# Float64 weights to float32 by a Prelu on ScalarE, with one VectorE operation a piece fewer

## The chip, the cores and the metric

One core of a Trainium2 chip runs the whole program. The metric is the device time of one execution in microseconds. Times of several runs are given by their median.

## The reference

The reference is a chain of three layers on 4 sequences of 576 tokens. The first is attention with 8 heads of 64 in a window of 32 keys (dilated by 4 in half of the heads). The second mixes with phases, the third is a gated unit whose gate runs over the tokens:

```python
theta = x @ w_theta
zr, zi = x * cos(theta), x * sin(theta)
u = x + w_tok_r @ zr + w_tok_i @ zi          # over the tokens
x = u + maximum(u @ w_ch, 0)
h = maximum(x @ w_in, 0); u, v = halves of h
v_n = (v - mean(v)) / sqrt(var(v) + 1e-6)
out = (u * (w_spatial @ v_n + b_spatial)) @ w_out
```

q, k, v, w_spatial and b_spatial are float32. w_theta, w_tok_r, w_tok_i, w_ch, w_in and w_out arrive as float64 and have to be brought to float32 on the chip.

## The kernel before

Matrix products run as float32r in three terms: each operand is split into a high part and a low part, and high x high, low x high and high x low are summed in PSUM. So each weight goes through three steps: float64 to float32 (bits64), a rounded copy as the high part, and a subtraction for the low part (split_weight, which L144 ends).

bits64 takes a piece of 128 rows by 256 or 288 columns. A DMA on SP's queue brings the 64-bit words to SBUF (four buffers named w64; w_theta has buffers of its own, wth64). The high words, read as float32 with a step of two, are multiplied by 2^-112, which moves the exponent to where float32 wants it (L128 on ScalarE or L130 on GpSimd, by a letter in a table). VectorE then does three operations: L131 shifts the low words right by 29 into c, which lies in PSUM; L132 shifts the scaled word left by 3 and ors c into it, again into c; L133 keeps the sign bit of the scaled word and ors c into it.

The letters of IN_ENG, SP_ENG, OUT_ENG, TOK_ENG, CH_ENG and THETA_ENG (L53 to L57) say which engine makes the high part, which the low part, and, as a third letter, which scales in bits64 (GpSimd where there is none). ScalarE scales the first half of w_tok (9 pieces), w_ch (8) and w_out (8); GpSimd scales w_theta (8), the second half of w_tok (9) and w_in (16).

The program is written as generators that are interleaved, and a scheduler in the tile framework then sets the order of the instructions on each engine; each engine's queue runs in that order. The stages are: attention of batch 0 (scores L250, exps L265, division L268 on GpSimd, transposes L278, their copies L280, values L292 and L296, and copies of the result into x, L299 to L308), with the w_theta pieces among it; the theta units of batch 0 (th_unit: xh L350, xl L353, twelve matmuls L358, ta L366, L367, Sin L375 and L376, products L379, then zh and zl by split, zl at L330 on GpSimd), with the first half of w_tok among them; token mixing of batch 0 (tm_run, L429 and L436) together with attention of batch 1, the second half of w_tok and w_ch; channel mixing (ch_run, L455); the same for the other batches with w_in among them; then the second half (hv_unit L650, hu_run L695, sp_run L714 to L717, out_unit L743), at whose start the w_out pieces are converted among the layer norms.

The tables and the place where w_theta is queued:

```python
IN_ENG, SP_ENG, OUT_ENG = "vgg", "ag", "aga"
TOK_ENG = ("aga", "gv")
CH_ENG = "vga"
THETA_ENG = "gg"
```

Of the kernel before, what the change touches and what calls it, by code (L numbers as in the profile page):

```python
# [11 lines left out]
F32 = mybir.dt.float32  # L12
# [3 lines left out]
AF = mybir.ActivationFunctionType  # L16
ALU = mybir.AluOpType
# [32 lines left out]
HELD = 2  # L50


IN_ENG, SP_ENG, OUT_ENG = "vgg", "ag", "aga"  # L53
TOK_ENG = ("aga", "gv")
CH_ENG = "vga"
THETA_ENG = "gg"
Z_HI = ("v", "g")  # L57

# [5 lines left out]
def tile_block(ctx: ExitStack, tc: tile.TileContext, qT, kT, vw, eye_in, mask_in, eye_b_in, w_theta, w_tok, w_ch, w_in, w_sp, w_sph, b_sp, w_out, out):  # L64
    nc = tc.nc
    V, A, G, PE, SY = nc.vector, nc.scalar, nc.gpsimd, nc.tensor, nc.sync

    def f32(ap):
        return ap.bitcast(F32)
# [34 lines left out]
    def copy(dst, src, eng):  # L104
        if eng == "a":
            A.copy(dst, src)  # L106
        elif eng == "v":
            V.tensor_copy(dst, src)
        else:
            G.tensor_scalar(dst, src, 1.0, 1.0, op0=ALU.mult, op1=ALU.mult)  # L110

    last_dma = [None]

    def bits64(src, n, eng, st=None):

        p = src.shape[0]
        if st is None:
            st = const.tile([P, 2 * CH], U32, tag="w64", name="w64", bufs=4)  # L120
        last_dma[0] = SY.dma_start(st[:p, :2 * n], src.bitcast(U32))
        w = st[:p, :2 * n].rearrange("p (n w) -> p n w", w=2)
        lw, hw = w[:, :, 0], w[:, :, 1]
        g = const.tile([P, CH], F32, tag="stage", name="w64g", bufs=4)[:p, :n]
        c = c64[:p, :n].bitcast(U32)
        gi = g.bitcast(U32)
        if eng == "a":
            A.mul(g, hw.bitcast(F32), 2.0**-112)  # L128
        else:
            G.tensor_scalar(g, hw.bitcast(F32), 2.0**-56, 2.0**-56, op0=ALU.mult, op1=ALU.mult)  # L130
        V.tensor_scalar(c, lw, 29, None, op0=ALU.logical_shift_right)  # L131
        V.scalar_tensor_tensor(c, gi, 3, c, op0=ALU.logical_shift_left, op1=ALU.bitwise_or)  # L132
        V.scalar_tensor_tensor(gi, gi, 0x80000000, c, op0=ALU.bitwise_and, op1=ALU.bitwise_or)  # L133
        return g

    def split_weight(src, hi, lo, eng_hi, eng_lo, eng_bits="g", st=None):
        n = hi.shape[-1]
        if src.dtype == F32:
            s = const.tile([P, CH], F32, tag="stage", name="stage", bufs=4)[:src.shape[0], :n]
            SY.dma_start(s, src)  # L140
        else:
            s = bits64(src, n, eng_bits, st)
        copy(hi, s, eng_hi)
        (G if eng_lo == "g" else V).tensor_tensor(lo, s, f32(hi), op=ALU.subtract)  # L144

    def halves(src, hi, lo, k, n, engs):

        for c in range(2):
            cs = slice(n // 2 * c, n // 2 * (c + 1))
            split_weight(src[:, k, cs], hi[:, k, cs], lo[:, k, cs], *engs)  # L150

    def stored(src, dst, k, cs, engs):

        n = cs.stop - cs.start
        t = const.tile([P, 2, CH], F32R, tag="parts", name="parts", bufs=2)[:, :, :n]
        split_weight(src[:, k, cs], t[:, 0], t[:, 1], *engs)
        SY.dma_start(f32(dst[:, k, :, cs]), f32(t))

    def w_theta_job(k, c):
        cs = slice(DM // 2 * c, DM // 2 * (c + 1))  # L160
        split_weight(w_theta[:, k, cs], wth_h[:, k, cs], wth_l[:, k, cs], *THETA_ENG, st=pz.tile([P, DM], U32, tag=f"z{'hl'[c]}{k}", name="wth64"))

    def w_tok_job(k, c):
        cs = slice(CH * c, CH * (c + 1))
        split_weight(w_tok[:, k, cs], wtok_h[:, k, cs], wtok_l[:, k, cs], *TOK_ENG[c])

    wch = []

    def w_ch_job(k):
        if not wch:  # L170
            wch.extend(p1.tile([P, 4, DM], F32R, tag=n, name=n) for n in ("wch_h", "wch_l"))
        halves(w_ch, *wch, k, DM, CH_ENG)

# [392 lines left out]
    n = 0  # L566
# [272 lines left out]
```

## Time and profile before

| | us |
|---|---|
| median of 3 runs | 552.2 |
| lowest and highest run | 551.26, 556.32 |
| span of the profiled execution | 552.0 |
| TensorE busy in it | 533.7 |
| VectorE busy | 318.1 |
| ScalarE busy | 246.1 |
| GpSimd busy | 262.9 |

The profiled execution is one of its own; the page gives its span, from the first instruction to the last, and no other time of it. The median of the runs stands 0.2 us above that span. In the profile's rows PE is TensorE, DVE is VectorE, ACT is ScalarE, POOL is GpSimd, SP is the engine whose queue issues DMAs. A time in brackets is the engine's idle time ahead of the instruction, with what ended it.

### The profile page before, as it was taken

The page shows a single profiled execution, that of the slowest core. Times are in us where ns is not written, and L with a number is a line of the kernel's source. Part 1 is how long each engine was busy: PE and PEld are TensorE (multiplying, and loading weights), DVE is VectorE, ACT ScalarE, POOL GpSimd, SP SyncE. Part 2 cuts the span into 40 slices and gives each one's busy share as a digit, 9 for nine tenths or more (in the row PEclk, how much of TensorE's full clock was granted, in tenths as well). Part 3 has the DMA queues.
Part 4 walks back from the last instruction along what each step waited for, and adds up shares of the span by engine and source line. Part 5 has one row for each costly group of instructions (what it writes and reads, how often), then busy time and mean ns, then how long its engine had stood idle before and what let it go on. Part 6 is the DMA issues. An engine that isn't in the chain of part 4 may idle for free.

```text
span 552.0 us, 11197 instructions
## 1 busy us (share of the span) xinstructions
PE 533.7 (97%) x4148; PEld 476.6 (86%) x4148; DVE 318.1 (58%) x834; ACT 246.1 (45%) x718; POOL 262.9 (48%) x333
## 2 busy tenths in 40 slices
PE   6897989999999999999999999989999999999997
PEld 4674878888989988889889999989899889988996
DVE  2688999899778378762782143984602148253020
ACT  4769855535655444772560124742422233233222
POOL 3484996554995249820296328563302204322040
PEclk9979899999999999999999999999999999999999
DMA  8925755662378552630006968250015110002002
GB/s 217 288 74 151 212 156 169 192 191 80 94 233 244 129 179 93 212 96 2 0 1 215 371 210 267 94 170 3 21 57 172 58 38 1 2 1 77 1 0 96
DMA packets 43759, 67.16 MB, mean 122 GB/s; under 512 B 3764, under 2 KB 26552, under 8 KB 43704
## 3 DMA queue, kind: packets, MB, share of 16 engines
q1 hardware_dynamic: 43480, 66.26, 39.0%
q8 instruction: 33, 0.54, 0.4%
q10 hardware_dynamic: 224, 0.18, 0.1%
q14 instruction: 22, 0.18, 0.1%
HBM read 48.08 MB, written 18.35 MB: 120 GB/s over the span
## 4 chain that ended last, share of the span: by engine, by line
PE 71%; DVE 10%; DMA 6%; ACT 5%; issue 4%; POOL 3%; SPq 1%; ACTq 0%; POOLq 0%; DVEq 0%
PE ps_y L436 18%; PE ps_o L743 9%; PE ps_sp L714 9%; PE ps_hu L695 7%; PE ps_hv L650 6%; PE ps_th L358 5%; PE ps_r L455 5%; PE s L250 3%; PE pt L278 3%; PE ps_x L292 2%; DMA wth<-w_theta 2%; DMA stage<-w_sp 1%; DMA qz_2wch_h<-qT 1%; PE ps_x L296 1%; ACT sm L265 1%
## 5 line engine op out<-in xcount | busy, mean ns | idle before, releaser
L436 PE MATMUL ps_y<-wtok_h,zh 128*128 128x288 f32 x270 | 81.6, 306 | 0.7 <-DVE sm L261 0.4
L436 PE MATMUL ps_y<-wtok_h,zl 128*128 128x288 f32 x270 | 80.5, 299 | 0.4 <-POOL zl L330 0.4
L436 PE MATMUL ps_y<-wtok_l,zh 128*128 128x288 f32 x270 | 79.4, 297 | 0.0
L330 POOL TENSOR_TENSOR gl<-hu,gh 128x288 fp32r<-128x288 f32 x32 | 26.0, 813 | 71.1 <-ACT gh L106 71.1
L436 PEld LDWEIGHTS ps_y<-wtok_h,zh 128*128 128x128 f32 x270 | 50.4, 188 | 3.1 <-DVE sm L261 0.9
L718 DVE TENSOR_TENSOR hu<-ps_sp,hu 128x288 f32<-128x288 f32 x32 | 14.6, 457 | 66.2 <-PE ps_sp L717 66.1
L436 PEld LDWEIGHTS ps_y<-wtok_h,zl 128*128 128x128 f32 x270 | 50.7, 188 | 1.7 <-POOL zl L330 0.8
L436 PEld LDWEIGHTS ps_y<-wtok_l,zh 128*128 128x128 f32 x270 | 50.4, 188 | 0.6
L268 POOL TENSOR_TENSOR sm<-sm,l 128x288 f32<-128x288 f32 x48 | 32.1, 674 | 36.7 <-DVE l L267 22.7
L330 POOL TENSOR_TENSOR vl<-hv,vh 128x512 fp32r<-128x512 f32 x16 | 21.0, 1317 | 51.7 <-ACT vh L106 46.5
L265 ACT ACTIVATE sm<-sm,m 128x96 f32<-128x96 f32 x108 | 39.2, 364 | 13.3 <-DVE m L262 8.1
L330 POOL TENSOR_TENSOR ul<-x,uh 128x288 fp32r<-128x288 f32 x32 | 26.7, 842 | 25.9 <-ACT uh L106 25.6
L714 PE MATMUL ps_sp<-wsp_h,vl 128*128 128x288 f32 x128 | 37.9, 296 | 0.6 <-POOL vl L330 0.6
L439 DVE TENSOR_TENSOR x<-ps_y,x 128x288 f32<-128x288 f32 x40 | 17.6, 449 | 35.6 <-PE ps_y L436 35.5
L714 PE MATMUL ps_sp<-wsp_h,vh 128*128 128x288 f32 x128 | 37.8, 296 | 0.0
L455 PE MATMUL ps_r<-uh,wch_h 128*128 128x288 f32 x128 | 37.6, 300 | 0.2 <-DVE x L439 0.2
L714 PE MATMUL ps_sp<-wsp_l,vh 128*128 128x288 f32 x128 | 37.8, 295 | 0.0
L695 PE MATMUL ps_hu<-x2h,win_h 128*128 128x288 f32 x128 | 37.7, 294 | 0.0
L695 PE MATMUL ps_hu<-x2h,win_l 128*128 128x288 f32 x128 | 37.7, 294 | 0.0
L695 PE MATMUL ps_hu<-x2l,win_h 128*128 128x288 f32 x128 | 37.7, 294 | 0.0
L455 PE MATMUL ps_r<-uh,wch_l 128*128 128x288 f32 x128 | 37.5, 296 | 0.0
L455 PE MATMUL ps_r<-ul,wch_h 128*128 128x288 f32 x128 | 36.7, 295 | 0.0
(183 smaller groups left out, 1581.3 us busy)
## 6 DMA issues: line engine op xcount, KB each, us to landing
x2d<-parts SPq DMA_DIRECT2D x32, 288.0 KB, 2.7
vt<-vw SPq DMA_DIRECT2D x16, 432.0 KB, 4.1
w<-w_tok SPq DMA_DIRECT2D x18, 288.0 KB, 2.9
x2h<-x2d SPq DMA_DIRECT2D x8, 576.0 KB, 10.2
x2l<-x2d SPq DMA_DIRECT2D x8, 576.0 KB, 10.4
kt<-kT SPq DMA_DIRECT2D x15, 304.0 KB, 3.7
w<-w_in SPq DMA_DIRECT2D x16, 256.0 KB, 2.9
win_d<-parts SPq DMA_DIRECT2D x16, 256.0 KB, 2.4
```

Source lines behind the costliest of these rows:

```text
L250: PE.matmul(o, qz[:, j, T * t:T * (t + 1)], kt[:, T * t:T * t + KW], start=not on_pe, stop=not on_pe)
L265: ia = A.activation(sm[:, t, :], src[:, t, :], AF.Exp, bias=m_[:, t:t + 1], scale=scale, accum_out=l[:, t:t + 1])
L268: ig = G.tensor_tensor(sm, sm, l.unsqueeze(2).to_broadcast([P, 3, KW]), op=ALU.mult)
L330: return (G if el == "g" else V).tensor_tensor(dst_l, src, f32(dst_h), op=ALU.subtract)
L358: PE.matmul(ps, lh[:, k, :], rh[:, k, :], start=(i == 0), stop=(i == 11))
L436: PE.matmul(ps[:, :CH], lh[b, k][:, P * d:P * (d + 1)], rh[:, k, cs], start=(n == 0), stop=(n == 3 * len(ks) - 1))
L439: V.tensor_tensor(xv, ps[:, :CH], xv, op=ALU.add)
L455: PE.matmul(ps[:, :CH], lh[:, k, P * e:P * (e + 1)], rh[:, k, cs], start=(n == 0), stop=(n == 11))
L650: PE.matmul(ps, lh[:, k, ts_], rh[:, k, DM:], start=(n == 0), stop=(n == 11))
L695: PE.matmul(ps[:, :CH], lh[:, k, fs], rh[:, k, cs], start=(n == 0), stop=(n == 11))
L714: PE.matmul(ps[:, :CH], lh[b, k][:, fs], rh[:, k, cs], start=(n == 0), stop=False)
L743: PE.matmul(ps, lh[:, k, ts_], rh[:, k, cs], start=(n == 0), stop=(n == 11))
```

## The change

Only ScalarE scales now, by an activation with the function Prelu. Prelu passes a positive value and multiplies a negative one by alpha; with alpha = 2^32 a negative word has its exponent raised by 32, which sets the bit that the shift by 3 moves to the sign's place. So the shifted word carries its sign, L133 is not needed, and the remaining operation writes the result over the scaled word. The third letter of the tables is gone: 33 pieces (w_theta, the second half of w_tok, w_in) are scaled on ScalarE instead of GpSimd.

```diff
-IN_ENG, SP_ENG, OUT_ENG = "vgg", "ag", "aga"
-TOK_ENG = ("aga", "gv")
-CH_ENG = "vga"
+IN_ENG, SP_ENG, OUT_ENG = "vg", "ag", "ag"
+TOK_ENG = ("ag", "gv")
+CH_ENG = "vg"
...
-        if eng == "a":
-            A.mul(g, hw.bitcast(F32), 2.0**-112)
-        else:
-            G.tensor_scalar(g, hw.bitcast(F32), 2.0**-56, 2.0**-56, op0=ALU.mult, op1=ALU.mult)
+        A.activation(g, hw.bitcast(F32), AF.Prelu, scale=2.0**-112, alpha=2.0**32)
         V.tensor_scalar(c, lw, 29, None, op0=ALU.logical_shift_right)
-        V.scalar_tensor_tensor(c, gi, 3, c, op0=ALU.logical_shift_left, op1=ALU.bitwise_or)
-        V.scalar_tensor_tensor(gi, gi, 0x80000000, c, op0=ALU.bitwise_and, op1=ALU.bitwise_or)
+        V.scalar_tensor_tensor(gi, gi, 3, c, op0=ALU.logical_shift_left, op1=ALU.bitwise_or)
         return g
```

Since the scheduler orders the instructions anew, much else moves. Lines below the edit are lower by 4 in the changed kernel (its Prelu is L127, its one VectorE operation L129).

ScalarE in the middle of the first attention, before (L265 are exps, L258 the scaling of the row maxima, L280 copies of transposed weights, L299 copies into x):

```order
L258 ACTIVATE m<-m 128x3
L265 ACTIVATE sm,l<-s,m 128x96 x3
L258 ACTIVATE m<-m 128x3
L280 COPY pT<-pt 96x384
L265 ACTIVATE sm,l<-s,m 128x96 x3
L258 ACTIVATE m<-m 128x3
L265 ACTIVATE sm,l<-s,m 128x96 x3
L258 ACTIVATE m<-m 128x3
L299 COPY x_138<-ps_x 128x384
```

ScalarE at the same place in the changed kernel:

```order
L254 ACTIVATE m<-m 128x3
L127 ACTIVATE w64g<-wth_331 128x256
L261 ACTIVATE sm,l<-s,m 128x96 x3
L254 ACTIVATE m<-m 128x3
L276 COPY pT<-pt 96x384
L127 ACTIVATE w64g<-wth_339 128x256
L127 ACTIVATE w64g<-wth_373 128x256
L261 ACTIVATE sm,l<-s,m 128x96 x3
L254 ACTIVATE m<-m 128x3
L127 ACTIVATE w64g<-wth_381 128x256
L127 ACTIVATE w64g<-wth_429 128x256
L254 ACTIVATE m<-m 128x3
```

Five w_theta pieces (wth) now stand among these exps; three more follow before the last copies into x.

ScalarE at the end of the first attention, before (L304 to L308 are the last two heads' copies into x, L350 the first xh of the theta units):

```order
L304 COPY x_138<-ps_x 128x2x144
L305 COPY x_138<-ps_x 128x96
L280 COPY pT<-pt 96x384
L307 COPY x_138<-ps_x 128x48
L308 COPY x_138<-ps_x 128x144
L280 COPY pT<-pt 96x384 x2
L304 COPY x_138<-ps_x 128x2x144
L305 COPY x_138<-ps_x 128x96
L307 COPY x_138<-ps_x 128x48
L308 COPY x_138<-ps_x 128x144
L350 ACTIVATE xh<-x_138 128x4x64
L350 ACTIVATE xh<-x_138 128x512
```

ScalarE at the same place in the changed kernel, from the fourth w_tok piece on (w_705 to w_805 are the fourth to seventh pieces of w_tok):

```order
L127 ACTIVATE w64g<-w_705 128x288
L106 CAST wtok_h<-w64g 128x288
L127 ACTIVATE w64g<-w_750 128x288
L300 COPY x_138<-ps_x 128x2x144
L301 COPY x_138<-ps_x 128x96
L127 ACTIVATE w64g<-w_758 128x288
L106 CAST wtok_h<-w64g 128x288
L127 ACTIVATE w64g<-w_805 128x288
L303 COPY x_138<-ps_x 128x48
L304 COPY x_138<-ps_x 128x144
L106 CAST wtok_h<-w64g 128x288
L346 ACTIVATE xh<-x_138 128x4x64
```

Seven of the nine w_tok pieces of the first half now come before the first xh; before, all nine came behind it.

GpSimd at the end of the theta units of batch 0, before (L144 are low parts of w_tok, L130 scalings, L110 high parts and L330 low parts of z):

```order
L144 TENSOR_TENSOR wtok_l<-w64g,wtok_h 128x288
L110 TENSOR_SCALAR zh_815<-ta 128x512
L330 TENSOR_TENSOR zl_811<-tb,zh_810 128x512
L330 TENSOR_TENSOR zl_816<-ta,zh_815 128x512
L144 TENSOR_TENSOR wtok_l<-w64g,wtok_h 128x288
L110 TENSOR_SCALAR zh_872<-ta 128x512
L330 TENSOR_TENSOR zl_873<-ta,zh_872 128x512
L130 TENSOR_SCALAR w64g<-w_989 128x288
L130 TENSOR_SCALAR w64g<-w_998 128x288
L330 TENSOR_TENSOR zl_868<-tb,zh_867 128x512
```

GpSimd at the same place in the changed kernel:

```order
L110 TENSOR_SCALAR zh_746<-spare 128x512
L326 TENSOR_TENSOR zl_742<-spare,zh_741 128x512
L326 TENSOR_TENSOR zl_747<-spare,zh_746 128x512
L110 TENSOR_SCALAR zh_801<-ta 128x512
L326 TENSOR_TENSOR zl_797<-tb,zh_796 128x512
L326 TENSOR_TENSOR zl_802<-ta,zh_801 128x512
L110 TENSOR_SCALAR zh_856<-ta 128x512
L326 TENSOR_TENSOR zl_857<-ta,zh_856 128x512
L326 TENSOR_TENSOR zl_852<-tb,zh_851 128x512
```

All nine low parts of w_tok's first half now stand ahead of the first zl, and no scaling is left between the zl.

## Rows read from the trace of the kernel before

**Rows 1.** The page, part 4: the chain that ended last, by engine.

```profile
PE 71%; DVE 10%; DMA 6%; ACT 5%; issue 4%; POOL 3%; SPq 1%; ACTq 0%; POOLq 0%; DVEq 0%
```

**Rows 2.** Stretches: length; busy PE, PEld, DVE, ACT, POOL; clock, DMA share, GB/s.

```profile
20.70:36.40 15.70, 13.56 (x171) 10.29 (x167) 11.53 (x33) 10.62 (x46) 12.30 (x25) 0.78 0.62 211
36.40:64.00 27.60, 23.82 (x126) 17.77 (x126) 23.84 (x48) 21.68 (x43) 17.74 (x20) 0.94 0.55 152
36.00:76.00 40.00, 34.69 (x230) 27.57 (x231) 35.31 (x77) 29.95 (x79) 29.60 (x35) 0.96 0.51 143
76.00:185.00 109.00, 108.98 (x1040) 95.95 (x1038) 92.31 (x249) 60.57 (x200) 69.85 (x99) 1.00 0.58 174
...
330.00:368.00 38.00, 36.61 (x229) 33.55 (x228) 27.95 (x82) 22.23 (x56) 26.04 (x30) 1.00 0.50 159
```

**Rows 3.** The chain that ended last, 76 to 185 us, by engine and line.

```profile
by line: PE ps_y L436 43.5%; PE ps_th L358 12.6%; PE ps_r L455 12.3%; PE s L250 11.3%; PE pt L278 8.0%; PE ps_x L292 6.6%; PE ps_x L296 3.2%; PE ps_xn L370 2.0%; ACT x L308 0.2%; PE ps_y L429 0.2%; ACT x L307 0.2%; issue 0.0%
```

**Rows 4.** Timeline of PE, 362 to 369 us: start, length, instruction, idle before.

```profile
365.94 0.40 PE L714 MATMUL ps_sp<-wsp_h,vl 128*128 128x288 f32 x1 [0.64 <-POOL vl L330]
...
367.35 0.40 PE L716 MATMUL ps_sp<-wsp_hh,vhl 128*128 128x288 f32 x1 [0.75 <-POOL vhl L678]
```

**Rows 5.** The chain that ended last, in order of time: start, length, what.

```profile
14.36 9.23 DMA wth<-w_theta
...
40.09 2.79 DMA w<-w_tok
...
54.72 4.37 PE ps_th L358 x11
...
120.20 10.95 PE ps_th L358 x48
```

**Rows 6.** Groups by form, DVE: count, busy us, mean ns of one, idle before.

```profile
L133 DVE SCALAR_TENSOR_TENSOR w64g<-w64g,c 128x256 uint32<-128x256 uint32 x40 | 16.6, 414 | 0.8
...
L133 DVE SCALAR_TENSOR_TENSOR w64g<-w64g,c 128x288 uint32<-128x288 uint32 x18 | 8.0, 445 | 0.3
```

**Rows 7.** Groups by form, ACT.

```profile
L376 ACT ACTIVATE tb<-tb,half_pi 128x512 f32<-128x512 f32 x15 | 10.6, 708 | 0.0
...
L375 ACT ACTIVATE ta<-ta 128x512 f32<-128x512 f32 x15 | 9.5, 631 | 11.5 <-DVE tb L374 11.3
...
L128 ACT ACTIVATE w64g<-w 128x256 f32<-128x256 f32 x16 | 7.0, 436 | 8.0 <-DMA w<-w_ch 4.0 <-DVE wtok_l L144 2.0 <-POOL wo_l L144 1.2
...
L375 ACT ACT_TABLE_LOAD x4 | 5.1, 1283 | 0.1
L128 ACT ACTIVATE w64g<-w 128x288 f32<-128x288 f32 x9 | 4.1, 461 | 2.4 <-POOL wth_l L144 2.4
...
L106 ACT CAST wtok_h<-w64g 128x288 fp32r<-128x288 f32 x9 | 3.8, 420 | 3.7 <-DVE w64g L133 3.7
```

**Rows 8.** Timeline of DVE, 20 to 76 us.

```profile
23.62 0.43 DVE L131 TENSOR_SCALAR c<-wth 128x256 uint32<-128x256 uint32 x1 [2.10 <-DMA wth<-w_theta]
```

**Rows 9.** Timeline of ACT, 20 to 76 us.

```profile
20.55 0.20 ACT L258 ACTIVATE m<-m 128x3 f32<-128x3 f32 x1
...
36.39 0.94 ACT L350 ACTIVATE xh<-x 128x256 fp32r<-128x256 f32 x2
37.23 0.81 ACT L128 ACTIVATE w64g<-w 128x288 f32<-128x288 f32 x2
...
63.95 1.28 ACT L265 ACT_TABLE_LOAD   x1
```

**Rows 10.** Timeline of POOL, 22 to 80 us.

```profile
66.83 0.81 POOL L144 TENSOR_TENSOR wtok_l<-w64g,wtok_h 128x288 fp32r<-128x288 f32 x1 [0.46 <-ACT wtok_h L106]
...
69.57 1.10 POOL L130 TENSOR_SCALAR w64g<-w 128x288 f32<-128x288 f32 x2
70.65 1.27 POOL L330 TENSOR_TENSOR zl<-tb,zh 128x512 fp32r<-128x512 f32 x1
```

**Rows 11.** Stretch 76 to 185 us, L133 alone: length, busy (count), clock, DMA, GB/s.

```profile
76.00:185.00 109.00, 11.82 (x28) 1.00 0.58 174
```

More of the change, by code (lines that the diff above doesn't have):

```diff
@@ L112, in tile_block, with bits64 @@
     last_dma = [None]
-    def bits64(src, n, eng, st=None):
+    def bits64(src, n, st=None):
         p = src.shape[0]
@@ L126, in bits64, with split_weight @@
         gi = g.bitcast(U32)
-        if eng == "a":
-            A.mul(g, hw.bitcast(F32), 2.0**-112)
-        else:
-            G.tensor_scalar(g, hw.bitcast(F32), 2.0**-56, 2.0**-56, op0=ALU.mult, op1=ALU.mult)
+        A.activation(g, hw.bitcast(F32), AF.Prelu, scale=2.0**-112, alpha=2.0**32)
         V.tensor_scalar(c, lw, 29, None, op0=ALU.logical_shift_right)
-        V.scalar_tensor_tensor(c, gi, 3, c, op0=ALU.logical_shift_left, op1=ALU.bitwise_or)
-        V.scalar_tensor_tensor(gi, gi, 0x80000000, c, op0=ALU.bitwise_and, op1=ALU.bitwise_or)
+        V.scalar_tensor_tensor(gi, gi, 3, c, op0=ALU.logical_shift_left, op1=ALU.bitwise_or)
         return g
-    def split_weight(src, hi, lo, eng_hi, eng_lo, eng_bits="g", st=None):
+    def split_weight(src, hi, lo, eng_hi, eng_lo, st=None):
         n = hi.shape[-1]
@@ L141, in split_weight @@
         else:
-            s = bits64(src, n, eng_bits, st)
+            s = bits64(src, n, st)
         copy(hi, s, eng_hi)
```

## The prediction

> **What bounds the kernel now.** I read the page's totals first (the table above): TensorE is busy 533.7 of 552.0 us, VectorE 318.1, ScalarE 246.1, GpSimd 262.9. Of the chain that ended last 71% is TensorE and 10% VectorE [rows 1], so an operation taken off VectorE is worth something only where TensorE waits for VectorE or for something queued behind it. The table by stretches says where [rows 2]:
>
> - 20.7 to 36.4 us, the tail of the first attention: TensorE idles 2.1 of 15.7 us, ScalarE 5.1.
> - 36.4 to 64.0 us, the theta units of batch 0: TensorE idles 3.8 of 27.6 us, while VectorE is busy 23.8 and ScalarE 21.7.
> - 36 to 76 us, the same and the start of token mixing: TensorE idles 5.3 of 40 us, VectorE only 4.7.
> - 76 to 185 us: TensorE is busy 108.98 of 109 us, although VectorE is busy 92.3, and the chain there is TensorE's almost alone [rows 3]. TensorE sets the pace.
> - 330 to 368 us, the entry to the second half: TensorE idles 1.4 of 38 us, both gaps for GpSimd: 0.64 for vl and 0.75 for vhl [rows 4].
>
> These idle times are a lower bound on what can be won: a matmul counts as busy until a modelled end, so a dependent one that starts late shows less idle time than it lost. Eleven theta matmuls on the chain from 54.72 us took 4.37 us (0.40 each), 48 of them from 120.20 us took 10.95 (0.23 each) [rows 5]. Part of that is the clock: the mean granted clock is 0.78 and 0.94 in the first two stretches [rows 2], so some of them ran at 1.2 GHz and not at 2.4, after the gaps that TensorE has there.
>
> **The change part by part.** There are 58 pieces of float64 weights: 8 of w_theta, 18 of w_tok, 8 of w_ch, 16 of w_in and 8 of w_out.
>
> VectorE loses one of three operations a piece. The one that goes writes c, and the one that stays has the operands of the old last one: 414 ns at 256 columns (40 pieces), 445 ns at 288 (18) [rows 6]. That is 40 x 0.414 + 18 x 0.445 = 24.6 us of VectorE's 318.
>
> ScalarE keeps its 25 scalings and gains GpSimd's 33 (8 w_theta, 9 w_tok, 16 w_in). A Prelu is not in the trace. The same read and write as an ACTIVATE with immediate operands is 436 ns at 256 columns and 461 at 288; with another function or a pointer bias, two rows of 512 columns stand at 631 and 708, so 0.08 us more is the upper bound, and the contiguous 420 ns cast of 288 columns the lower [rows 7]. I take 436 and 461, the rows nearest in shape: 24 x 0.436 + 9 x 0.461 = 14.6 us more on ScalarE. GpSimd loses about as much. No table load is added: the order of the change has nine, like before. The trace prices one at 1283 ns [rows 7].
>
> The Trainium skill (ScalarE: Activation LUTs, Table sets: the hidden batching unit) says that functions of different sets cost a reload at every switch, and its list of the fillers that are in every set does not name Prelu; no run here shows Prelu yet, and the built order speaks against a reload (it is the last rival below).
>
> Early stretch, a loss. In the new order ScalarE's first w_theta Prelu stands ahead of three exps, right after the small m scaling that ends at 20.75 us in the trace. Its data lands 9.23 us after 14.36, so at 23.6 [rows 5]. VectorE already waits 2.10 us for the same transfer [rows 8]; now ScalarE waits 2.9 too, with exps behind it. Between there and the first xh the new order has 8 w_theta and 7 w_tok Prelus and 5 wtok_h casts that were not there: 8 x 0.436 + 7 x 0.461 + 5 x 0.42 = 8.8 us, or some 7.0 when they follow each other closely (two scalings in a row took 0.81 us, 0.1 less than twice one [rows 9]). ScalarE was busy 10.62 of that stretch [rows 2]. So xh can start at 20.7 + 2.9 + 10.6 + 7.0 = 41.2 us at the best and at 43.0 without overlap, instead of 36.39 [rows 9]. I take 41.5: 5.1 us late. What waits behind those instructions: the copies of the last head's x, the transposes' copies, then xh and through it every theta matmul.
>
> Theta units, a gain. ScalarE's 21.7 busy us of this stretch held 9 scalings and 6 casts of w_tok (9 x 0.461 + 6 x 0.42 = 6.7 us); 2 and 4 stay there (2.6 us). 21.7 - 6.7 + 2.6 = 17.6 us of work, plus 2 us of waits for TensorE and VectorE (it idled 5.9 before), gives the last Sin at 41.5 + 19.6 = 61.1 us. Before it ended just ahead of the table load at 63.95 [rows 9], and the last zl followed at 70.65 + 1.27 = 71.9 us, 8.0 us later. In these 8.0 us GpSimd waited 0.46 us for a w_tok cast, made one wtok_l (0.81) and two scalings (1.10) [rows 10]; the new order has none of them there, so 5.6 us remain and the last zl comes at 61.1 + 5.6 = 66.7 us, 5.2 earlier. VectorE does not stand against that: it was busy 35.3 of the 40 us from 36 to 76, and now most of the first half of w_tok lies ahead of the stretch and each piece is a third shorter. I take 5.2 us for TensorE, whose products in token mixing need every zl.
>
> 76 to 330 us: w_tok's second half, w_ch and w_in. TensorE is busy to 0.02 us of 109, so I count zero, although VectorE sheds up to 28 operations or 11.8 us there [rows 11] and ScalarE gains the 18 or so scalings that GpSimd made. Cover gone: 12 w_in Prelus each behind a 2.8 us transfer [rows 5] in front of exps could cost 2 us; fewer hand-overs could save as much or more (second rival).
>
> 330 to 368 us: the 8 w_out pieces stood between the layer-norm operations on VectorE: 8 x 0.414 = 3.3 us off the way to vl and vhl, worth the two gaps of 1.4 us in all [rows 4]; behind them TensorE has only its own queue.
>
> Sum for the profiled execution: 552.0 - 5.2 - 1.4 = 545.4 us. Its span stands 0.2 us under the median of the three runs (552.2), so the same number serves for the time, 6.8 us or 1.2% less.
>
> **Rivals.**
>
> *The early delay eats the gain (no change).* If ScalarE keeps waiting in the theta units as it did (5.9 us idle instead of 2) and xh comes at 43.0, the last zl is at 66.7 + 3.9 + 1.5 = 72.1 us, 0.2 later than before; with the 1.4 us won later the time is 550.8. For it: the units form a chain matmul, ta, Sin, product, zl, which has latency whatever ScalarE's load is. Against it: the 2.4 us that GpSimd sheds at the end of that chain hold in any case.
>
> *VectorE is the second bound also from 76 to 185 us (faster still).* Weight loads are busy 95.95 of 109 us there and VectorE 92.3 [rows 2]; if half of these 13 us of loose packing go with VectorE's load, 6.5 us more: 538.9. Against it: the chain there [rows 3].
>
> *ScalarE stands still behind transfers (slower).* Four w_tok pieces have buffers; the fifth to seventh transfers start only when a buffer is read, and their Prelus now stand ahead of the last x copies. A transfer on the chain took 2.79 us [rows 5]. If each of the three costs its whole transfer, xh comes 8.4 us later than I take; TensorE, idle so long, starts the units at the lower clock: 24 matmuls at 0.40 instead of 0.23 are 4 us. Then 545.4 + 8.4 + 4 = 557.8. The change is slower from the point where waits and lower clock together exceed 6.6 us. Against it: they follow each other by only a Prelu or two, so they would mostly overlap.
>
> *A table load at each switch (slower).* With Prelu outside the loaded set, every run of pieces among exps would pay 2 x 1.283 us; some 40 runs give 103 us, about 650. The nine loads in the built order say no.
>
> **How the numbers follow.** The forecast, 545.4, has 0.42; its own range is 542 to 548.5 (the Prelu's 0.08 us bound over the 15 early ones is 1.2 us, the overlap of ScalarE's instructions 1.8). Faster still (538.9): 0.20. No change (550.8): 0.25. Standing still (557.8): 0.12, the table loads 0.01. About 1%, 5.5 us, is what a measurement tells from no change here, so the line is at 546.7: of the forecast's 0.42 I put 0.38 below it. Faster 0.20 + 0.38 = 0.58, same 0.25 + 0.04 = 0.29, slower 0.13. The range for 8 in 10 runs from 534 (the faster rival with three quarters of the loose packing gone instead of half) to 556 (short of the full three waits).
>
> **What would show it.** Right: the Prelus at 0.43 to 0.47 us; nine table loads; VectorE near 293 us busy, ScalarE near 261, GpSimd near 248; first xh at 41 to 43 us; the Exp table load after the theta units at 61 to 63 us; last zl of batch 0 near 66 to 68 us; 76 to 185 us with the same matmuls in the same length, only earlier; the vl and vhl gaps gone. Wrong: xh after 46 us or the last zl after 71 (ScalarE stood still), or a stretch from 76 to 185 us that shrinks by over 3 us (VectorE was the bound after all), or Prelus of over 0.55 us.

## The result: 0.7% slower, not 1.2% faster

The changed kernel takes 556.97 us (median of 14 runs, 554.05 to 559.29), the kernel before 552.89 beside it (14 runs). The ratio is 1.0069, 95% interval [1.0045, 1.0092]. The forecast was 545.4 with a range up to 556.

The profiled run of the changed kernel took 555.8 us, with a span of 554.0: 2.0 us more than the span of before. Its totals, from the page:

```profile
PE 533.6 (96%) x4148; PEld 477.0 (86%) x4148; DVE 304.4 (55%) x777; ACT 254.2 (46%) x750; POOL 247.5 (45%) x300
PEclk9958999999999999999999999999999999999999
```

VectorE and GpSimd shed work, ScalarE gained some, and TensorE's own work is the same to 0.1 us. So the 2 us are waits and clock. The Prelus and the VectorE operation that stays, from the groups by form (they answer to [rows 6] and [rows 7]):

```profile
L127 ACT ACTIVATE w64g<-w 128x256 f32<-128x256 f32 x32 | 13.8, 434 | 12.4 <-DMA w<-w_ch 6.4 <-POOL parts L140 2.3 <-DMA w<-w_out 0.9
...
L127 ACT ACTIVATE w64g<-w 128x288 f32<-128x288 f32 x18 | 8.0, 466 | 2.8 <-DMA w<-w_tok 1.4 <-DVE wtok_l L140 1.3
...
L127 ACT ACTIVATE w64g<-wth 128x256 f32<-128x256 f32 x8 | 3.4, 454 | 2.8 <-DMA wth<-w_theta 2.4 <-POOL wth_l L140 0.3
```

```profile
L129 DVE SCALAR_TENSOR_TENSOR w64g<-w64g,c 128x256 uint32<-128x256 uint32 x40 | 16.5, 411 | 5.0 <-ACT w64g L127 4.0
...
L129 DVE SCALAR_TENSOR_TENSOR w64g<-w64g,c 128x288 uint32<-128x288 uint32 x18 | 8.0, 446 | 1.4 <-ACT w64g L127 0.6
```

The prices were right: 434 to 466 ns for a Prelu, 411 and 446 for the operation that stays. The table loads are still nine. The stretches, to be laid beside [rows 2] (columns: length, then busy time and count of PE, PEld, DVE, ACT, POOL, then clock, DMA share, GB/s):

```profile
20.70:36.40 15.70, 12.49 (x142) 9.41 (x141) 12.33 (x37) 12.69 (x54) 11.93 (x22) 0.75 0.67 226
36.00:76.00 40.00, 36.87 (x267) 30.16 (x268) 31.43 (x63) 31.06 (x78) 26.47 (x30) 0.88 0.55 152
76.00:185.00 109.00, 107.16 (x1040) 94.56 (x1036) 81.11 (x217) 65.67 (x221) 60.67 (x78) 1.00 0.57 170
185.00:230.00 45.00, 43.32 (x359) 38.71 (x355) 32.97 (x68) 21.08 (x54) 26.89 (x30) 1.00 0.45 139
330.00:368.00 38.00, 37.73 (x239) 34.78 (x239) 27.56 (x76) 21.53 (x55) 24.49 (x30) 1.00 0.45 138
```

Two things are to be seen. In the first two stretches the clock is lower than before (0.75 and 0.88; before 0.78 and 0.96). And from 76 to 185 us, where TensorE had idled 0.02 us of 109, it now idles 1.84, although VectorE is busy 81.1 us there and not 92.3. What TensorE waited for from 76 to 232 us in the changed kernel (us in total, times, longest):

```profile
PE ps_x L288 <- ACT pT L276: 0.8, 1, 0.8
PE ps_y L432 <- DVE sm L257: 0.8, 1, 0.8
PE ps_y L432 <- POOL zl L326: 0.5, 1, 0.5
PE ps_r L451 <- DVE ta L363: 0.5, 1, 0.5
PE ps_r L451 <- DVE x L454: 0.4, 1, 0.4
PE s L246 <- DVE sm L257: 0.2, 1, 0.2
PE pt L274 <- ACT x L295: 0.2, 1, 0.2
```

The same query of the kernel before has two rows:

```profile
PE ps_y L436 <- DVE sm L261: 0.4, 1, 0.4
PE ps_y L436 <- POOL zl L330: 0.4, 1, 0.4
```

The theta units, on ScalarE (to [rows 9]):

```profile
23.82 0.44 ACT L127 ACTIVATE w64g<-wth 128x256 f32<-128x256 f32 x1 [2.44 <-DMA wth<-w_theta]
...
41.41 0.46 ACT L127 ACTIVATE w64g<-w 128x288 f32<-128x288 f32 x1 [1.29 <-DMA w<-w_tok]
...
42.40 0.95 ACT L346 ACTIVATE xh<-x 128x256 fp32r<-128x256 f32 x2
...
61.37 0.69 ACT L362 ACTIVATE ta<-ps_th,magic 128x512 f32<-128x512 f32 x1 [2.20 <-PE ps_th L354]
...
64.94 0.71 ACT L372 ACTIVATE tb<-tb,half_pi 128x512 f32<-128x512 f32 x1
...
67.10 1.28 ACT L261 ACT_TABLE_LOAD   x1
```

and the last zl of batch 0 on GpSimd (to [rows 10]):

```profile
58.87 0.73 POOL L110 TENSOR_SCALAR zh<-spare 128x512 fp32r<-128x512 f32 x1 [2.86 <-DVE spare L375]
...
70.82 1.30 POOL L326 TENSOR_TENSOR zl<-tb,zh 128x512 fp32r<-128x512 f32 x1
```

and GpSimd alone between these two (length, busy and count, then clock, DMA share, GB/s):

```profile
58.87:72.12 13.25, 12.80 (x13) 1.00 0.24 70
```

xh starts at 42.40 us, 0.9 later than forecast; the last zl ends at 72.12, not at 66.7, and 0.2 us after that of before. From 58.87 us, when the first products of 128 rows reach it, GpSimd is busy 12.80 of 13.25 us up to that end, with high and low parts of z alone. The first of the losses is there, the gain that was to pay for it isn't.

To place the 2 us, I count for each moment the matmuls that TensorE has started, each with the usual interval between two of its line (0.13 us for one of 288 columns), and compare with before at the same moment. This is an estimate worked out from the traces, and another choice of the usual interval moves a difference by up to 0.6 us; a minus is work that TensorE is behind. The last three columns are experiments told of below (the second run of the 50, and the piece of w_tok):

```
us    work in before   changed   all 58, old order   50, old order   one piece
 50        34.4          -5.2          -3.4              -1.6           -1.8
 80        56.9           0.0          -1.8               0.0           -1.3
140       113.0          +1.4          -1.4              +0.3           -0.5
180       151.8          -0.6          -1.7              -0.7           -2.0
230       199.4          -1.7          -1.4              -0.5           -1.7
330       297.0          -2.0          -1.4              -0.7           -1.7
400       364.6          -2.1          -0.7              +0.2           -3.6
```

In this execution of the changed kernel the 5.2 us lost by 50 us are made up by 80. What stays lost is lost from 140 to 230 us.

### The profile page after: what moved, and what is told of

Its sections match the earlier page's. It is cut to its first block, busy times and chain, and to the rows that moved or that the text cites. A ratio compares the mean times of both kernels' runs of the same rounds, so it can differ in the third digit from the quotient of the medians.

```text
span 554.0 us, 11128 instructions
## 1 busy us (share of the span) xinstructions
PE 533.6 (96%) x4148; PEld 477.0 (86%) x4148; DVE 304.4 (55%) x777; ACT 254.2 (46%) x750; POOL 247.5 (45%) x300
## 5 line engine op out<-in xcount | busy, mean ns | idle before, releaser
L714 DVE TENSOR_TENSOR hu<-ps_sp,hu 128x288 f32<-128x288 f32 x32 | 14.6, 457 | 66.4 <-PE ps_sp L713 66.3
```

The source lines that it names most:

```text
L714: V.tensor_tensor(t[:, f, cs], ps[:, :CH], t[:, f, cs], op=ALU.mult)
```

## The experiments

The first theories: the late xh and the low clock after it (one), the w_in Prelus on ScalarE from 140 to 230 us (two), the scheduler's new order as such (three).

**Parts of the change, each ordered anew.** The saving alone (25 pieces):

```diff
-IN_ENG, SP_ENG, OUT_ENG = "vgg", "ag", "aga"
-TOK_ENG = ("aga", "gv")
-CH_ENG = "vga"
+IN_ENG, SP_ENG, OUT_ENG = "vgg", "ag", "agp"
+TOK_ENG = ("agp", "gv")
+CH_ENG = "vgp"
...
+        if eng == "p":
+            A.activation(g, hw.bitcast(F32), AF.Prelu, scale=2.0**-112, alpha=2.0**32)
+            V.tensor_scalar(c, lw, 29, None, op0=ALU.logical_shift_right)
+            V.scalar_tensor_tensor(gi, gi, 3, c, op0=ALU.logical_shift_left, op1=ALU.bitwise_or)
+            return g
```

> Prelu and two VectorE operations only for the 25 pieces that ScalarE scaled already (first half of w_tok, w_ch, w_out); GpSimd scales its 33 as before, with three operations. So VectorE sheds 16 x 0.414 + 9 x 0.445 = 10.6 us and nothing moves to ScalarE. Theories one and two (the loss comes from work moved into ScalarE's queue, early or among the exps from 140 us on): first xh back at 36 to 37 us, no loss from 140 to 230 us, the two gaps of 1.4 us at 366 us gone; 550 to 552 us, 0.1 to 0.4% under before. Theory three (the scheduler's new order as such costs 2 to 4 us, whatever moved): 0.3 to 0.8% over before, with the loss at places that have nothing to do with a scaling.

Measured: 556.54 us, ratio 1.0066 [1.0036, 1.0097]. Nothing was moved to ScalarE, and nearly the whole loss is there. Theory two can't make that, and theory one not as a cost of moved work; but the first xh was late here too, at 39.21 us where 36 to 37 was expected.

The changed kernel with w_theta back on GpSimd. "p" stands for a Prelu and two VectorE operations; all other letters of the changed kernel stay:

```diff
-THETA_ENG = "ggp"
+THETA_ENG = "gg"
```

> The changed kernel, but with w_theta's 8 pieces scaled on GpSimd and finished with three operations, as before; with that the pieces of w_tok, too, leave the place ahead of the first xh on ScalarE. Theory one (late first xh and the half clock from 28.5 to 45.6 us are the cause, some 5 us of TensorE work missing at 50 us): first xh at 36 to 37.5 us, half clock as short as before, and 3 to 5 us less than the changed kernel, 0.2% over to 0.3% under before. Theory two (the w_in pieces on ScalarE from 140 to 230 us are the cause, the early loss being won back by 120 us): within 1.5 us of the changed kernel, 0.4 to 0.9% over before, and the loss from 140 to 230 us still there.

Measured: 557.1 us, 1.0073 [1.0043, 1.0103]. xh started at 35.41 us, so theory one had its way with the early stretch, and the time did not follow. Instead TensorE waited elsewhere. ScalarE at 99 to 104 us in this run, then TensorE:

```profile
99.30 0.44 ACT L128 ACTIVATE w64g<-w 128x256 f32<-128x256 f32 x1 [2.91 <-DMA w<-w_ch]
101.61 0.43 ACT L128 ACTIVATE w64g<-w 128x256 f32<-128x256 f32 x1 [1.88 <-DMA w<-w_in]
...
103.82 0.46 ACT L285 COPY pT<-pt 96x384 f32<-96x384 f32 x1
```

```profile
104.33 0.57 PE L301 MATMUL ps_x<-pT,vt 96*64 96x64 f32 x12 [1.87 <-ACT pT L285]
```

Two Prelus stand in ScalarE's queue ahead of exps and of a pT copy and wait 2.91 and 1.88 us for their transfers; TensorE then waits 1.87 us for that copy. That is the rival of the prediction in which ScalarE stands still behind transfers, at a place that the prediction had counted at zero.

With w_in back on GpSimd:

```diff
-IN_ENG, SP_ENG, OUT_ENG = "vgp", "ag", "agp"
+IN_ENG, SP_ENG, OUT_ENG = "vgg", "ag", "agp"
```

> The changed kernel, but with w_in's 16 pieces scaled on GpSimd and finished with three operations, as before. Theory one (the early stretch): first xh stays at 42 to 43 us and the time stays within 1.5 us of the changed kernel, 0.4 to 0.9% over before. Theory two (w_in among the exps on ScalarE): the 3.5 us lost from 140 to 230 us do not appear, 2 to 4 us less than the changed kernel, 0.3% over to 0.2% under before. Theory three (the new order as such): 0.3 to 0.8% over before with the loss somewhere else.

Measured: 554.77 us, 1.0035 [1.0007, 1.0064]; with both of these edits:

> Both at once: w_theta's 8 and w_in's 16 pieces on GpSimd with three operations, all else as in the changed kernel (34 pieces with Prelu). Theory one alone: as the run with w_theta alone. Theory two alone: as the run with w_in alone. Both: the gains add up, first xh at 36 to 37.5 us and no loss from 140 to 230 us, 547 to 551 us, 0.3 to 1% under before. Theory three: 0.3 to 0.8% over before.

Measured: 555.34 us, 1.0057 [1.0027, 1.0087]. The two do not add up, and neither comes under before. The move without the saving (all 58 pieces by ScalarE's old multiply, three VectorE operations):

```diff
-IN_ENG, SP_ENG, OUT_ENG = "vgp", "ag", "agp"
-TOK_ENG = ("agp", "gvp")
-CH_ENG = "vgp"
-THETA_ENG = "ggp"
+IN_ENG, SP_ENG, OUT_ENG = "vga", "ag", "aga"
+TOK_ENG = ("aga", "gva")
+CH_ENG = "vga"
+THETA_ENG = "gga"
```

> The move without the saving: ScalarE scales all 58 pieces with its old multiply, VectorE keeps three operations, the scheduler orders anew. Theory that the move into ScalarE's queue costs: 0.5 to 1.2% over before, the clock at half speed for as long as in the changed kernel. Theory of the order: some other order and so some other time, between 0.3% under and 1% over before, with its waits at other places than the changed kernel's.

Measured: 554.97 us, 1.0048 [1.0020, 1.0075]. Every part, and the opposite parts, cost 0.3 to 0.7%. TensorE's waits from 76 to 232 us are partly others than those of the changed kernel: all five of these programs have one that it lacks, for transposes that are reached before GpSimd has divided (pt for sm, 0.2 to 2.6 us in total). That speaks for the order.

**The order held fixed.** Here each engine's instructions are tied in the order of the kernel before, by edges that set the order of issue and make nothing wait for an end:

```diff
...
+    for seq in order:
+        seq = [n for n in seq if n in traced]
+        for a, b in zip(seq, seq[1:]):
+            tc.add_manual_dep(traced[b], traced[a].name, info, reason="pin")
```

In the built programs TensorE's list is then that of before, instruction for instruction. The saving alone in this order:

> The operations of the run with the saving alone (25 pieces with Prelu and two VectorE operations, GpSimd's 33 with three), but every engine's instructions stand in the order of the kernel before, written out as ordering edges; only the 25 VectorE operations are missing. Theory of the order (the scheduler answers to the shorter VectorE work with another order on every engine, TensorE's too, and that order costs 3 to 5 us): the loss goes, and the gaps of 1.4 us at 366 us go too: 0.1 to 0.6% under before, 549.5 to 552 us. Theory of the work (Prelu or the missing operation do harm as such, by what they set free earlier): still 0.3 to 0.8% over before.

> The saving alone (25 pieces) in the order of the kernel before, once more beside the two runs above, to tell whether it is faster than before: 0.4 to 0% under before, gaps at 366 us gone, everything else where it was.

Measured: 551.71 us, 0.9982 [0.9945, 1.0019], and again 551.48 us, 0.9978 [0.9944, 1.0013]. The same operations that cost 0.66% in the scheduler's order cost nothing in the old one. In the second run TensorE is as full from 76 to 185 us as before:

```profile
76.00:185.00 109.00, 109.00 (x1040) 96.44 (x1041) 88.33 (x239) 60.57 (x201) 69.27 (x98) 1.00 0.58 172
```

The converse, the operations of before in the order made for the saving alone:

> The converse: the operations of the kernel before, all three on VectorE, in the order that the scheduler gave to the run with the saving alone. Theory of the order: 0.4 to 1% over before, as that run or more, since this order was made for less VectorE work, and the two gaps at 366 us back. Theory of the work: within 0.3% of before.

Measured: 561.12 us, 1.0160 [1.0115, 1.0205]. Nothing but places in queues differs from the kernel before. From 76 to 185 us, and the longest wait later on:

```profile
76.00:185.00 109.00, 106.23 (x996) 92.28 (x997) 92.60 (x240) 57.80 (x191) 68.09 (x97) 1.00 0.58 168
```

```profile
366.26 0.51 PE L695 MATMUL ps_hu<-x2h,win_h 128*128 128x288 f32 x1 [2.86 <-ACT hv L653]
```

TensorE idles 2.77 us in the first stretch. The 2.86 us later were not expected there (the two gaps for vl and vhl were): this order counted on shorter w_out pieces, so the run says more than that of an order alone. The kernel before with its own order written out by such edges was not run; this run shows that the edges alone do not make a program fast.

All operations of the changed kernel in the order of before, each moved Prelu where GpSimd's scaling stood in time:

> All operations of the changed kernel (58 Prelus on ScalarE, two VectorE operations a piece), in the order of the kernel before; each of the 33 Prelus that came from GpSimd stands in ScalarE's queue where the scheduler had GpSimd's scaling in time. Theory of the order: at or under before, 0 to 0.6% under. Theory that the move into ScalarE's queue costs (theories one and two of before: transfers waited for ahead of exps and copies): 0.2 to 0.6% over before, with ScalarE waiting for w_theta, w_tok and w_in transfers and the first xh late by 2 us or more.

Measured: 554.36 us, 1.0025 [0.9997, 1.0054]. Without the reordering 0.25% is left of 0.69%, with an interval that reaches just under 1. It is lost early: ScalarE waits for w_theta with exps behind it, and xh starts at 40.07 us; from 76 to 185 us TensorE never idles, w_in Prelus or not:

```profile
26.07 0.43 ACT L128 ACTIVATE w64g<-wth 128x256 f32<-128x256 f32 x1 [2.74 <-DMA wth<-w_theta]
...
40.07 0.92 ACT L356 ACTIVATE xh<-x 128x256 fp32r<-128x256 f32 x2
```

```profile
76.00:185.00 109.00, 109.00 (x1032) 96.26 (x1032) 81.99 (x222) 67.89 (x228) 62.97 (x84) 1.00 0.61 177
```

So in the old order the same with w_theta left on GpSimd (50 Prelus; first edit), and with w_theta alone moved (33 Prelus; second edit, from the 25):

```diff
-THETA_ENG = "ggp"
+THETA_ENG = "gg"
...
-THETA_ENG = "gg"
+THETA_ENG = "ggp"
```

> In the order of the kernel before: all Prelus but w_theta's (50 pieces; w_theta's 8 stay on GpSimd with three VectorE operations). If the cost of the move lies in w_theta's Prelus, which stand among the exps of the first attention and ahead of the last x copies: as the run with the saving alone in the old order, 0.4% under to 0.1% over before, and TensorE no more than 0.7 us behind before from 80 us on. If it lies in w_in or w_tok: 0.1 to 0.5% over before, with the loss from 76 us on.

> 50 Prelus in the order of the kernel before, once more: 0.1 to 0.4% under before; with the first run of it an interval that lies under before.

> In the order of the kernel before: the 25 pieces of the saving alone and w_theta's 8 on ScalarE (33 Prelus); w_in and the second half of w_tok stay on GpSimd with three VectorE operations. If w_theta's Prelus carry the cost of the move: 0.1 to 0.5% over before, TensorE 1 to 2 us behind before at 70 us, the same at 330 us. If w_in's or w_tok's do: 0.4% under to 0.1% over before.

Measured for 50 Prelus: 551.24 us, 0.9981 [0.9960, 1.0002], and again 551.63 us, 0.9955 [0.9922, 0.9988]; for 33 with w_theta: 552.35 us, 1.0005 [0.9976, 1.0033]. The move of w_in and w_tok costs nothing in the old order. That of w_theta costs 0.44% from the 50 (first run; 0.70% from the second) to all 58, and 0.23% from the 25 to the 33; only the interval of the second run of the 50 lies clear of its partner's. The 33 came out level with before, where 0.1 to 0.5% over was expected, and by the count above TensorE was 0.4 us behind at 80 us and level at 330, not 1 to 2 us behind. The version with 50 Prelus in the old order stands some 1% under the changed kernel (by the ratios to before), and under before by 0.2 and 0.45%, in the second run with an interval under 1, though the medians there, 551.63 and 552.42 us, are only 0.14% apart. In the stretch from 76 to 185 us its second run had one new wait, 0.9 us (pt for sm), and TensorE busy 108.13 of 109 us.

**One piece.** How much does it take to lose the order? The kernel before, with one piece of the 58 done in the new way (eng is "a" for the 25 pieces that ScalarE scales; ONE is 2, the second piece of w_tok, then 10 and 14, the first and the fifth of w_ch):

```diff
+        ones[0] += eng == 'a'
+        if eng == 'a' and ones[0] == ONE:
+            A.activation(g, hw.bitcast(F32), AF.Prelu, scale=2.0**-112, alpha=2.0**32)
...
+            return g
```

> The kernel before with a single piece (the second one of w_tok) done with Prelu and two VectorE operations, everything else as it was, ordered anew by the scheduler: 0.4 us of VectorE's work less, and 735 of TensorE's 3598 instructions in another place. Theory of the order: the time moves by more than 0.4 us, by 0.3 to 0.8% either way, most likely up. Theory of the work: within 0.15% of before.

> The kernel before with another single piece (the first of w_ch) done with Prelu and two VectorE operations, ordered anew: 460 of TensorE's instructions in another place. Theory of the order (that of before is a lucky one among many, and nearly any other costs): 0.2 to 0.7% over before. If new orders fall to either side by chance: as likely 0.2 to 0.5% under before. Theory of the work: within 0.15%.

> The kernel before with the fifth piece of w_ch alone done with Prelu and two VectorE operations, ordered anew: 437 of TensorE's instructions in another place, all late in the first half. As for the run before it: 0.2 to 0.7% over before if nearly any other order costs, either side if by chance, within 0.15% by the theory of the work.

Measured: 555.13 us, 1.0051 [1.0027, 1.0075]; 554.02 us, 1.0031 [1.0008, 1.0054]; 553.70 us, 1.0031 [1.0002, 1.0060]. 0.4 us less of VectorE's work makes the kernel 1.3 to 2.3 us slower, three times of three. Counted by their place in the built programs, 361, 203 and 174 of TensorE's 3596 matmuls and weight loads stand elsewhere than before, fewer than the expectations say. One wait of TensorE is common to the three, the transposes of attention reached before GpSimd has divided; the rows are from the timelines of the three runs, in the order above:

```profile
173.69 0.53 PE L286 MATMUL pt<-ident,sm 128*96 128x128 f32 x3 [0.67 <-POOL sm L276]
```

```profile
170.05 0.53 PE L286 MATMUL pt<-ident,sm 128*96 128x128 f32 x3 [1.30 <-POOL sm L276]
```

```profile
174.36 0.53 PE L286 MATMUL pt<-ident,sm 128*96 128x128 f32 x3 [0.88 <-POOL sm L276]
```

Neither before nor the changed kernel has this one; the changed kernel has the seven of its list above. The five programs of the first group have it. Taken together, TensorE's busy time from 76 to 185 us, one profile each:

| order | TensorE busy of 109 us |
|---|---|
| old: before; 25 pieces twice; 58; 50 twice; 33 | 108.98; 108.99, 109.00; 109.00; 108.87, 108.13; 108.99 |
| new: changed; 25 pieces; w_theta back; w_in back; both back | 107.16; 107.28; 105.77; 106.86; 105.46 |
| new: move alone; one piece, three times | 107.06; 108.00, 106.99, 107.73 |
| of the 25 pieces, with the operations of before | 106.23 |

Idle time in this stretch is not all time lost: with w_theta back, or both back, TensorE is 1.6 to 1.8 us ahead of before at 80 us by the count of matmuls, and part of its waiting only uses that up. By the same count the nine newly ordered programs fall back against before by 0.9 to 2.7 us between 140 and 180 us, and the six runs in the old order by at most 1.0, five of them by at most 0.6 (estimates). One profile does not size a loss more finely: at 330 us the runs with w_in back, with both back and with the first piece of w_ch are level with before to 0.1 us, though their times are 0.3 to 0.6% over.

## Why the prediction was wrong

**The theta units** ("I take 5.2 us for TensorE"). This is the first step that failed. The early loss was sized well (xh at 42.40 for 41.5). But the waits of ScalarE in the units were put at 2 us and came to 4.9, of which 3.2 for the theta matmuls (busy it was 18.4 us where 17.6 was forecast); the last Sin ended at 65.65 us, not 61.1. And from the last Sin to the last zl the sum gave 5.6 us, as if GpSimd then had only what that Sin released; it took 6.5, for GpSimd was full from 58.87 us on. So it went as the first rival said: the last zl at 72.1, 0.2 later than before. That its number fits to the tenth is partly luck: xh came 0.6 us earlier than there, ScalarE waited less than its 5.9 us, and the end took longer. Here a queue with less work in it did not go faster through a chain whose links are on other engines. At 80 us TensorE stands where it stood before: the term is 0, not -5.2.

**76 to 330 us** ("so I count zero"). This is the second step that failed, and in the profiled executions it decides the sign: 2.0 us lost. The argument was that TensorE has its work there and waits for no one. That held for the old order alone. The order of the built program was read at the places that the sum spoke of, and not on TensorE in this stretch; between before and the changed kernel 714 of its 3596 matmuls and weight loads stand elsewhere, and there it now reaches attention's steps and the phases before they are ready. In the old order the zero is right: with all 58 Prelus TensorE was busy 109.00 of 109 us. The second rival, VectorE as the bound, falls with that run too: 81.99 us of VectorE's work instead of 92.31, and TensorE gained 0.4 us on before from 80 to 330 us, not 6.5. The third rival, slower, lies near the measured time with its 557.8, but by luck: of its 8.4 us of waits for w_tok ahead of xh 1.4 came. So the last zl after 71 us, which the prediction named as a sign of a ScalarE that stands still, came for another reason.

**330 to 368 us** ("the two gaps of 1.4 us in all"). The gap for vl went, that for vhl stayed, and there is a new one:

```profile
PE ps_sp L712 <- POOL vhl L674: 0.9, 1, 0.9
PE ps_hu L691 <- ACT hv L649: 0.3, 1, 0.3
```

1.2 us instead of 1.4. In the old order the two gaps came to 0.9 and 0.3 us (25 pieces), 0.8 (58), 1.4 and 0.6 (50), and none (33): mostly shorter, seldom gone. They are GpSimd's, and less work on VectorE only helps where VectorE was last.

**The sum.** 0 + 2.0 - 0.2 against the span's 2.0; the account is good to some tenths. The medians differ by 4.1 us, more than the spans: the profiled run of after lay 1.2 us under its median, and that of before, with the 1.8 us around a span that the runs show, 0.9 over its own. So 545.4, worked out from that span, was set against other runs' median. Part of the rest is the clock, for which the sum had no term. The runs of the changed kernel show a mean granted clock of 0.985, those of before 0.993 (35 runs of another comparison). Among those, five at 1.000 have a mean span of 548.5 us and eight at 0.991 one of 551.4; by that 0.008 are some 2.6 us (an estimate). TensorE stands idle more in the first attention (12.49 us busy of 15.7 instead of 13.56), and the clock after it is at 1.2 GHz for longer (0.50 from 32 to 44 us, where before has 0.68 up to 36 us and 1.00 from there to 52).

In either order the clock is lower when ScalarE scales w_theta: in a new order 0.985, 0.985 and 0.988 with it and 0.990 to 0.994 without, in the old one 0.990 and 0.991 with it and 0.993 to 0.994 without. At the rate above that is 2.0 to 2.7 us of the 2.0 to 4.1 that the first three lose, but at most 1.0 of the 1.3 to 4.3 that the six other newly ordered programs lose (estimates). So a new order costs time at the clock of before too. How much of the changed kernel's own 4.1 us is clock and how much waits stays open: its profile is level with before at 80 us in spite of the clock. That the clock causes w_theta's share was not tried by itself.

In parts: the saving is worth about 0.2% (25 pieces, old order; both intervals reach past 1); moving w_in and w_tok costs nothing; moving w_theta costs 0.2 to 0.4% (0.7% against the second run of the 50), the rival of transfers in its small form; and the new order costs the rest, 0.44% from 1.0025 to 1.0069, with intervals that just overlap, and with a clock that falls from 0.990 to 0.985 in it. That a new order costs is shown by itself where nothing was moved: 0.66% against -0.2% for the same 25 pieces. Nine of nine programs that the scheduler ordered anew were 0.3 to 0.7% slower than before. What stays open is why that of before is so good; none of the nine escaped this price.

**Right:** the price of the Prelu and of the VectorE operation that stays, nine table loads, xh, and GpSimd's busy time (248 forecast, 247.5 measured). ScalarE came to 254.2 us where 261 was forecast, VectorE to 304.4 where 293 was. Instructions of one engine overlap, so a sum of durations counts too much: ScalarE's durations add up to 14.4 us more than before (14.6 was forecast), but its busy time, which counts an overlap once, grew by 8.1. VectorE's add up to 18.7 us less and its busy time fell by 13.7. And other VectorE operations took longer than before: L370, the same 14 operations as L374 of before, 662 ns each instead of 546, and the 16 casts to parts 496 instead of 376, 3.6 us together:

```profile
L370 DVE TENSOR_SCALAR tb<-ta 128x512 uint32<-128x512 uint32 (+1 forms) x14 | 9.3, 662 | 0.3
...
L108 DVE CAST parts<-w64g 128x256 fp32r<-128x256 f32 x16 | 7.9, 496 | 5.3 <-DMA x2d<-parts 2.7 <-DMA win_d<-parts 2.6
```

What they met there was not tried.

## What to carry to other kernels

Where a scheduler sets the order, a change of one operation is two changes: the operation and the order. Compare the built order on the engine that is full, over the whole stretch, and not only where the edited lines are; then run the new operations once in the old order, and the sign of each part can be read. Work that is put into a queue ahead of exps or copies should have its data there already: a Prelu of 0.44 us held ScalarE for 1.9 to 2.9 us.

## What was not expected of the hardware

The clock of the first 60 us is not the same from run to run of one program. The 25 pieces in the old order, profiled twice, had a granted clock of 0.79 and 1.00 from 20 to 44 us and of 1.00 and 0.89 from 44 to 60, and 1.00 after that in both. The 35 runs of before in one comparison have mean granted clocks from 0.984 to 1.000 and spans from 547.4 to 554.1 us, and the lower the clock the longer the span. A single profile of this kernel is thus good to some 3 us either way, hardly less than the whole effect of 4.1 us, which is why the ratios above rest on twelve runs each (14 for the changed kernel, six for the converse).

And a Prelu costs what the multiply cost: 434 and 466 ns for 436 and 461 (454 for w_theta's pieces).
